# Low parts, conversion ends and splits go from GpSimd to VectorE in the network stage of an attention, expert and feed-forward kernel

## The chip, the cores and the metric

The kernel runs on 1 core of one Trainium2 chip. The metric is the device time of one execution in microseconds (us). Engines are named as in the profile: PE is TensorE's matmul, PEld its weight load, DVE is VectorE, ACT is ScalarE, POOL is GpSimd, SP is the engine that issues most DMAs (SPq is its queue of issues).

## What is computed

Three parts in a row, in float32, and the change touches the last one only:

```python
attn_out = _attn_ref(q, k, v, tau)                  # (4, 8, 576, 64), thresholded softmax
x = attn_out.transpose(0, 2, 1, 3).reshape(2304, 512)
x = _moe_ref(x, expert_emb, tau, w1, w2)            # one of 8 experts per token
def _moe2_ref(x, w_in, w_out, alpha):               # w_in 512 x 2048, w_out 2048 x 512
    h = x @ w_in
    g = np.maximum(h, 0.0) + alpha * np.minimum(h, 0.0)
    return (g @ w_out).astype(np.float32)
```

## The kernel before, in words

PE works here on float32 that is rounded to a shorter form (fp32r). To keep precision every operand is held as two such numbers: the **high part** is a cast (ACT), the **low part** is the operand less its high part, a subtraction. A product is then three matmuls: high by high, high by low, low by high.

The attention and the experts fill the first 608 us of the profiled execution and are not touched. The network stage, `near_network` (line 1804), is the rest. It makes six **visits** (`VISITS`, line 52), numbered 0 to 5: three blocks of 768 tokens, each with two halves of the 2048 hidden units, in an order that changes the block between visits 0 and 1, 1 and 2, 3 and 4, 4 and 5. A visit has four **passes** `i` (0 to 3). In a pass, seven products `p` in the order 1, 2, 6, 7, 5, 3, 4 (Strassen-like, `prod`, line 1877, six matmuls of 384 columns each) give four tiles of h. They go into two PSUM banks, `ha` and `hb`; between products ACT copies a partial sum out of `ha` (`held`, line 1890, tiles `v`, `w`, `d`), and the next product that accumulates into `ha` waits for that copy. `act` (line 1898) makes g from the sums with ACT and DVE, `halves` casts it (`gh`, line 1927), `low` subtracts on POOL (`gl`, line 1932), and `f2mm` (line 1979) multiplies by w_out.

Beside this three kinds of work prepare what comes later, each a **chain** of steps:

- `wout` and `win` (lines 2010 and 2037) convert float64 weights that are loaded as `cr`: `cvsteps` (line 1609) has ACT and DVE steps and, for w_out, two POOL steps at the end (lines 1627 and 1628); `win` ends with an addition on POOL (line 2053).
- `factors(i)` (line 2064), i from 4 to 7, makes the weight operands of visits 3 to 5 for one pass each: it loads `wa`, makes four sums on DVE (line 1698), and then for seven products a cast on ACT (line 2084), a low part on POOL (line 2088) and a store of the tile `wf` to `ws` in HBM (line 2090). `wf` has three buffers, so the fourth cast waits until the store of the first tile has landed, and so on.
- `fetch`, `diff` and `split` load the next block of tokens and make its seven operands x: `xsplit` (line 2101) casts on ACT and subtracts two halves on DVE or POOL.

The program's order is made while it is built. `tick(us)` (line 1846) is called after every product and every `f2mm`. It gives each engine `us` of room, up to a ceiling of 1.2, and lets chains take steps in the order of their rank (g first, then stores, fetch and x, then conversions, last the factors) as long as the step's engine has room left; a step takes its stated cost off the room. `finish(name)` (line 1836) puts all the steps that a chain still has into the program at once. `prod` calls it for factors when the next weight load, five products ahead, would need them:

```python
            if y2["wnext"][0] < len(y2["wseq"]):
                vv, ii, _ = y2["wseq"][y2["wnext"][0]]
                finish(("f", VISITS[vv][1] * NQH + ii))
            y2["weights"]()
```

Each engine executes its instructions in the order in which they were put, and SP issues DMAs in that order too: weight loads `wr<-ws`, the fetches `raw<-yt_d`, the loads `cr` and the stores `ws<-wf` share its queue.

Of the kernel before, what the change touches and what calls it, by code (L numbers as in the profile page):

```python
# [10 lines left out]
F32 = mybir.dt.float32  # L11
# [5 lines left out]
ALU = mybir.AluOpType  # L17
# [4 lines left out]
B, H, S, D = 4, 8, 576, 64  # L22
# [27 lines left out]
PROD = (1, 2, 6, 7, 5, 3, 4)  # L50
# [162 lines left out]
def attn_moe_ffn(ctx: ExitStack, tc, q, k, v, tau, emb, mtau, w1, w2, w_in, w_out, alpha, out):  # L213
    nc = tc.nc
# [134 lines left out]
    add = plan.add  # L349
# [1218 lines left out]
    def shared(st, general):  # L1568
# [37 lines left out]
            nc.sync.dma_start(raw.rearrange("p (k f) -> p k f", k=k) if k > 1 else raw, cvsource(which, c))  # L1606
            CV[which, c] = raw

        def cvsteps(raw, f, r, hl):

            raw = raw.rearrange("p (n w) -> p n w", w=2)
            lo, hi = raw[:, :, 0], raw[:, :, 1]
            ff, rf = f.bitcast(F32), r.bitcast(F32)
            A, V, G = nc.scalar, nc.vector, nc.gpsimd
            yield "A", 0.67, lambda: A.activation(ff, hi.bitcast(F32), AF.Abs)
            yield "V", 0.75, lambda: V.tensor_scalar(out=ff, in0=ff, scalar1=F64_TINY, scalar2=None, op0=ALU.max)
            yield "V", 0.75, lambda: V.tensor_scalar(out=f, in0=f, scalar1=3, scalar2=0x3FFFFFFF,
                                                     op0=ALU.logical_shift_left, op1=ALU.bitwise_and)
            yield "V", 1.2, lambda: V.scalar_tensor_tensor(out=f, in0=hi, scalar=0xC0000000, in1=f, op0=ALU.bitwise_and,
                                                           op1=ALU.bitwise_or)  # L1620
            if hl is not None:
                yield "A", 0.65, lambda: A.copy(hl[:, 0, :], ff)
            yield "V", 0.5, lambda: V.tensor_scalar(out=r, in0=f, scalar1=0xFF800000, scalar2=None, op0=ALU.bitwise_and)
            yield "V", 0.75, lambda: V.scalar_tensor_tensor(out=rf, in0=lo, scalar=2.0 ** -52, in1=rf, op0=ALU.mult,
                                                            op1=ALU.mult)
            if hl is not None:
                yield "P", 1.55, lambda: G.tensor_tensor(ff, ff, hl[:, 0, :].bitcast(F32), op=ALU.subtract)
                yield "P", 1.4, lambda: G.tensor_tensor(hl[:, 1, :], ff, rf, op=ALU.add)

        def conv():  # L1630

# [172 lines left out]
    def near_network(y2):  # L1804
# [41 lines left out]
        def tick(us):  # L1846

            now[0] += 1
            for e in room:
                room[e] = min(room[e] + us, 1.2)  # L1850
            for x in list(chains):
                last = None
                while x["steps"] and x["at"] < now[0]:
                    e, cost, fn = x["steps"][0]
                    if last not in (None, e) or room.get(e, 1) <= 0 or e == "W" and not fn():
                        break
                    x["steps"].pop(0)
                    if e == "W":
                        continue
                    fn()  # L1860
                    if e in room:
                        room[e] -= cost
                    last = e
                    if e == "N":
                        break
                if last is not None:
                    x["at"] = now[0]
                if not x["steps"] and x in chains:
                    chains.remove(x)
# [140 lines left out]
        def wout(c):  # L2010

            x = {}

            def load():
                open_.append(c)
                x["raw"] = raw = cw_p.tile([128, 1024], U32, tag="cr", name="cr", bufs=2)
                nc.sync.dma_start(raw, y2["cvsource"](2, c))

            def begin():
                f, r = (cw_p.tile([128, 512], U32, tag=nm, name=nm, bufs=2) for nm in ("f", "r"))  # L2020
                if c < NWO:
                    WO[c] = wo_p.tile([128, 2, DM], F32R, tag=f"wo{c}", name=f"wo{c}")
                else:
                    WO[c] = y2["cvp"].tile([128, 2, DM], F32R, tag=f"wo{c - NWO}", name=f"wo{c}", bufs=1)
                x["steps"] = [y[2] for y in y2["cvsteps"](x["raw"], f, r, WO[c])]
                x["steps"][0]()

            def nth(k):
                x["steps"][k]()
                if k == 8:  # L2030
                    open_.remove(c)

            kinds = [("V", 0.75), ("V", 0.75), ("V", 1.2), ("A", 0.65), ("V", 0.5), ("V", 0.75), ("P", 1.55), ("P", 1.4)]
            chain(3, [("W", 0, lambda: len(open_) < 2), ("S", 0, load)] + [("N", 0, nothing)] * 3 + [("A", 0.67, begin)]
                  + [(e, t, lambda k=k: nth(k + 1)) for k, (e, t) in enumerate(kinds)], ("wo", c))

        def win(c):

            x = {}

            def load():
                open_.append(("c", c))
                x["raw"] = raw = cw_p.tile([128, 1024], U32, tag="cr", name="cr", bufs=2)
                nc.sync.dma_start(raw.rearrange("p (k f) -> p k f", k=2), y2["cvsource"](1, c))

            def begin():
                f, r = x["fr"] = [cw_p.tile([128, 512], U32, tag=nm, name=nm, bufs=2) for nm in ("f", "r")]
                x["steps"] = [y[2] for y in y2["cvsteps"](x["raw"], f, r, None)]
                x["steps"][0]()

            def add():
                f, r = (t.bitcast(F32) for t in x["fr"])
                P.tensor_tensor(f, f, r, op=ALU.add)

            def store():
                i, half = divmod(c, 2)
                nc.sync.dma_start(wa_d[i - NQH][:, half * DM:(half + 1) * DM], x["fr"][0].bitcast(F32))
                open_.remove(("c", c))

            chain(3, [("W", 0, lambda: len(open_) < 2), ("S", 0, load)] + [("N", 0, nothing)] * 3 + [("A", 0.67, begin)]  # L2060
                  + [("V", t, lambda k=k: x["steps"][k + 1]()) for k, t in enumerate((0.75, 0.75, 1.2, 0.5, 0.75))]
                  + [("P", 1.4, add), ("N", 0, nothing), ("S", 0, store)], ("c", c))

        def factors(i):

            x = {}

            def load():
                made.append(i)
                for c in (2 * i, 2 * i + 1):  # L2070
                    finish(("c", c))
                x["wa"] = wa = y2["wa"].tile([128, 2, DM], F32, tag="wa", name="wa")
                nc.sync.dma_start(wa.rearrange("p x n -> p (x n)"), wa_d[i - NQH])

            def nth(k):
                if k == 0:
                    x["sums"] = y2["sums"](i, x["wa"])
                x["sums"][k](V)

            def next_(k):  # L2080

                if k < 7:
                    x[k] = t, _, _ = y2["wtile"](y2["wf"], "wf", i, PROD[k])
                    A.copy(t[:, 0].rearrange("p (k j) -> p k j", k=2), SUM[i][PROD[k]])
                    did("A", 0.42)
                if 1 <= k < 8:
                    h, l = (x[k - 1][0][:, y].rearrange("p (k j) -> p k j", k=2) for y in range(2))
                    P.tensor_tensor(l, SUM[i][PROD[k - 1]], h.bitcast(F32), op=ALU.subtract)
                if k >= 2:
                    nc.sync.dma_start(x[k - 2][2], x[k - 2][1])  # L2090
                if k == 8:
                    made.remove(i)

            steps = [("W", 0, lambda: not made and not any(x["name"] in (("c", 2 * i), ("c", 2 * i + 1)) for x in chains)),
                     ("S", 0, load)] + [("N", 0, nothing)] * 3
            steps += [("V", 0.8, lambda k=k: nth(k)) for k in range(4)] + [("N", 0, nothing)]
            for k in range(9):
                steps += [("P", 0.95, lambda k=k: next_(k))] + [("N", 0, nothing)] * (k % 2)
            chain(4, steps, ("f", i))

        def xsplit(p, e):
# [12 lines left out]
        def after(v, i, p):  # L2114

            if moving(v):
# [4 lines left out]
                if i == NQH - 1:  # L2121
                    finish("fetch")
                    if p in (1, 2, 6):
                        xsplit(p, {1: "V", 2: "P", 6: "V"}[p])
                    if p == 2:
                        chain(2, [("N", 0, nothing), ("P", 1.1, x4), ("P", 1.1, lambda: diff(4, P, 1))], ("d", 4))
                    if p == 7:
                        xsplit(7, "V")
                    if p == 5:
                        xsplit(5, "P")  # L2130
                    if p == 3:
                        xsplit(3, "V")
                    if p == 4:
# [2 lines left out]

        def x4():
            finish(("x", 1))
            diff(4, P, 0)

        work = {0: [("o", NV, 0), ("o", NV + 1, 0), ("o", NV + 2, 1), ("o", NV + 3, 2)],
                1: [("f", NQH, 0), ("c", 2 * NQH + 4, 0), ("f", NQH + 1, 1), ("c", 2 * NQH + 5, 1), ("o", 8, 2)],
# [1 line left out]
                    ("o", 11, 2), ("o", 12, 3)],  # L2144
                3: [("o", 13, 0), ("o", 14, 1), ("o", 15, 2)]}

        xsplit(3, "V")
        xsplit(4, "V")
        for v, (q, h) in enumerate(VISITS):
            for i in range(NQH):  # L2150
                pair = h * NQH + i
# [218 lines left out]
```

## Time and profile before

| | |
|---|---|
| time, median of 3 runs | 1007.3 us (1006.34 to 1008.09) |
| the profiled execution | 1008.7 us |
| its span, first to last instruction | 1006.9 us |
| PE busy over the span | 960.2 us (95%) |
| DVE busy | 811.4 us (81%) |
| ACT busy | 633.0 us (63%) |
| POOL busy | 673.3 us (67%) |

The busy share of PE says little about stalls of a microsecond: the ends of matmuls are modelled, and what counts is where PE waited, for what, and at which granted clock.

### The profile page before, as it was taken

What the parts mean: (1) busy time and instruction counts of PE and PEld (TensorE: products, weight loads), DVE (VectorE), ACT (ScalarE), POOL (GpSimd) and SP (SyncE); (2) the same over time, 40 slices, a digit from 0 to 9 for tenths busy, and PEclk for the clock granted to TensorE, in tenths of its full rate; (3) what the DMA queues carried; (4) which work ended last, traced back from release to release, by engine and by line L of the source; (5) the groups of instructions that cost most, each with busy time, mean ns of one, the idle gap of its engine ahead of it and who ended that gap; (6) DMA issues with size and microseconds to landing.
All of it is one profiled execution on the core that took longest, in us unless ns stands there. A gap on an engine that the chain in (4) does not pass through costs nothing. (4 is left out here: it accounts for less than half of the span.)

```text
span 1006.9 us, 18456 instructions
## 1 busy us (share of the span) xinstructions
PE 960.2 (95%) x6099; PEld 889.6 (88%) x6099; DVE 811.4 (81%) x1461; ACT 633.0 (63%) x1451; POOL 673.3 (67%) x663
## 2 busy tenths in 40 slices
PE   7999999899999599999998999999989999999996
PEld 6899999799999499999997997888878888898895
DVE  7999999999999767969889776886877879746543
ACT  6999989799998444646555565575665625526220
POOL 6989899899999601745778564574765857735523
PEclk9999999999999799999999899999999999999998
DMA  2333455535452286887878687558677676574551
GB/s 75 104 97 83 131 165 177 157 101 143 123 146 80 108 304 200 293 282 229 299 246 245 211 226 229 160 175 297 197 251 242 203 257 199 161 236 146 178 168 67
DMA packets 119451, 186.08 MB, mean 185 GB/s; under 512 B 24056, under 2 KB 50968, under 8 KB 119344
## 3 DMA queue, kind: packets, MB, share of 16 engines
q1 hardware_dynamic: 115472, 174.48, 55.8%
q0 software_dynamic: 3456, 9.59, 2.5%
q8 instruction: 51, 0.84, 0.4%
q10 hardware_dynamic: 416, 0.72, 0.2%
q14 instruction: 56, 0.46, 0.2%
HBM read 127.48 MB, written 48.41 MB: 175 GB/s over the span
## 5 line engine op out<-in xcount | busy, mean ns | idle before, releaser
L1932 POOL TENSOR_TENSOR gl<-c,gh 128x384 fp32r<-128x384 f32 x96 | 110.1, 1150 | 134.6 <-ACT gh L1927 100.1
L446 POOL TENSOR_TENSOR ptl<-x,pth 128x512 fp32r<-128x512 f32 x97 | 124.8, 1287 | 6.8
L650 DVE SCALAR_TENSOR_TENSOR p<-s,mx,e 128x576 f32<-128x576 f32 x144 | 116.6, 812 | 7.5 <-ACT mx L638 3.2
L1225 PE MATMUL l<-x,w 128*128 128x256 f32 (+6 forms) x744 | 120.0, 311 | 0.0
L1883 PE MATMUL ha<-x,wr 128*128 128x384 f32 x576 | 117.3, 338 | 2.8 <-ACT c L1910 2.2
L1999 PE MATMUL o<-wo,gh 128*128 128x512 f32 x288 | 113.3, 393 | 2.4 <-ACT gh L1927 2.4
L2001 PE MATMUL o<-wo,gl 128*128 128x512 f32 x288 | 114.3, 397 | 1.1 <-POOL gl L1932 1.1
L634 DVE TENSOR_REDUCE mx<-s 128x1 f32<-128x576 f32 x144 | 108.5, 754 | 8.1 <-PE s L627 4.9
L2000 PE MATMUL o<-wo,gh 128*128 128x512 f32 x288 | 114.0, 396 | 0.0
L663 PE MATMUL t<-ident,p 128*128 128x128 f32 (+1 forms) x720 | 111.9, 276 | 2.3 <-ACT x L689 1.0
L1883 PEld LDWEIGHTS ha<-x,wr 128*128 128x128 f32 x576 | 103.1, 188 | 12.1 <-ACT c L1910 2.7
L1225 PEld LDWEIGHTS l<-x,w 128*128 128x128 f32 x744 | 112.1, 190 | 0.6
L643 ACT ACTIVATE e<-s,mx 128x576 f32<-128x576 f32 x144 | 106.3, 739 | 7.2 <-DVE mx L634 6.0
L663 PEld LDWEIGHTS t<-ident,p 128*128 128x128 f32 (+1 forms) x720 | 80.8, 137 | 8.5 <-DVE p L650 2.3
L1883 PE MATMUL hb<-x,wr 128*128 128x384 f32 x432 | 87.8, 338 | 0.5 <-DVE c L1905 0.5
L1208 ACT ACTIVATE h<-l 128x256 fp32r<-128x256 f32 (+6 forms) x64 | 28.2, 441 | 95.2 <-PE l L1225 90.4
L1257 PE MATMUL y<-h,w 128*128 128x256 f32 (+6 forms) x256 | 80.7, 315 | 5.5 <-DVE h L1209 5.3
L627 PE MATMUL s<-ks,qs 128*128 128x288 f32 x256 | 82.7, 338 | 3.0 <-ACT qs L534 1.4
L1256 PE MATMUL y<-h,w 128*128 128x256 f32 (+6 forms) x256 | 82.7, 323 | 0.6 <-ACT h L1208 0.6
L1138 POOL TENSOR_TENSOR w<-stg,w 128x512 fp32r<-128x512 f32 x28 | 38.4, 1371 | 65.6 <-ACT w L1137 62.3
L1258 PE MATMUL y<-h,w 128*128 128x256 f32 (+6 forms) x256 | 79.8, 312 | 0.0
L1883 PEld LDWEIGHTS hb<-x,wr 128*128 128x128 f32 x432 | 76.9, 190 | 1.5 <-DVE c L1905 1.5
(277 smaller groups left out, 2689.3 us busy)
## 6 DMA issues: line engine op xcount, KB each, us to landing
wr<-ws SPq DMA_DIRECT2D x168, 256.0 KB
stg<-in_moe_w_dram SPq DMA_DIRECT2D x34, 512.0 KB
stg<-in_moe_w_dram SPq DMA_DIRECT2D x15, 1024.0 KB
kx<-ks SPq DMA_DIRECT2D x60, 144.0 KB
xd<-zt SPq DMA_DIRECT2D x33, 256.0 KB
raw<-yt_d SPq DMA_DIRECT2D x10, 768.0 KB
ws<-wr SPq DMA_DIRECT2D x28, 256.0 KB
ws<-wf SPq DMA_DIRECT2D x28, 256.0 KB
```

The lines of the kernel that those rows point to most:

```text
L446: lambda: nc.gpsimd.tensor_tensor(lo, raw, hi.bitcast(F32), op=ALU.subtract))
L627: nc.tensor.matmul(s[:, hf, 0:288], lt, st[nm, a][:, hf * 288:(hf + 1) * 288], start=(j == 0 and x == 0), stop=(j == n - 1 and x == 1))
L634: nc.vector.tensor_reduce(out=mx[:, 0:1], in_=st["s", t][:, :, 0:288], op=ALU.min, axis=AX.XY)
L643: nc.scalar.activation(e, st["s", t][:, :, 0:288], AF.Exp, bias=st["mx", t][:, 0:1], scale=-1.0)
L650: nc.vector.scalar_tensor_tensor(out=p.rearrange("q (a b) -> q a b", a=2), in0=st["s", t][:, :, 0:288], scalar=st["mx", t][:, 2:3], in1=st ...
L663: nc.tensor.transpose(m[0:w, j * n + i * 128:j * n + (i + 1) * 128], st["p", t][:, c * 128:c * 128 + w], ident)
L1225: nc.tensor.matmul(m[:, 0:n], w[:, a, c], st["x"][:, b, c, 0:n], start=(i == 0), stop=(i + 1 == len(terms)))
L1883: nc.tensor.matmul(m, w[:, a, k], x[:, b, k], start=start and n == 0, stop=n + 1 == len(terms), skip_group_check=not start)
L1932: P.tensor_tensor(gl, c, gh.bitcast(F32), op=ALU.subtract)
L1999: nc.tensor.matmul(m, gh[:, ts], WO[f][:, 0, :], start=first and x == 0, stop=False)
L2000: nc.tensor.matmul(m, gh[:, ts], WO[f][:, 1, :], start=False, stop=False)
L2001: nc.tensor.matmul(m, gl[:, ts], WO[f][:, 0, :], start=False, stop=n[0] == full and x + 1 == len(gs))
```

## The change

Every subtraction or addition that POOL did for conversions, for factors and for the splits and differences of x in the network stage is put on DVE; the stated costs of these steps go down. POOL keeps `low` (gl) and the stores of the result by index. The ceiling of the room goes from 1.2 to 2.1. The splits of x 3 and 4 ahead of the first visit are finished before the first product is put.

```diff
-        def cvsteps(raw, f, r, hl):
+        def cvsteps(raw, f, r, hl, end="P"):
...
-            A, V, G = nc.scalar, nc.vector, nc.gpsimd
+            A, V = nc.scalar, nc.vector
+            G = V if end == "V" else nc.gpsimd
...
-                yield "P", 1.55, lambda: G.tensor_tensor(ff, ff, hl[:, 0, :].bitcast(F32), op=ALU.subtract)
-                yield "P", 1.4, lambda: G.tensor_tensor(hl[:, 1, :], ff, rf, op=ALU.add)
+                yield end, 1.55, lambda: G.tensor_tensor(ff, ff, hl[:, 0, :].bitcast(F32), op=ALU.subtract)
+                yield end, 1.4, lambda: G.tensor_tensor(hl[:, 1, :], ff, rf, op=ALU.add)
...
-                room[e] = min(room[e] + us, 1.2)
+                room[e] = min(room[e] + us, 2.1)
...
-                x["steps"] = [y[2] for y in y2["cvsteps"](x["raw"], f, r, WO[c])]
+                x["steps"] = [y[2] for y in y2["cvsteps"](x["raw"], f, r, WO[c], "V")]
...
-            kinds = [("V", 0.75), ("V", 0.75), ("V", 1.2), ("A", 0.65), ("V", 0.5), ("V", 0.75), ("P", 1.55), ("P", 1.4)]
+            kinds = [("V", 0.75), ("V", 0.75), ("V", 1.2), ("A", 0.65), ("V", 0.5), ("V", 0.75), ("V", 0.65), ("V", 0.65)]
...
-                P.tensor_tensor(f, f, r, op=ALU.add)
+                V.tensor_tensor(f, f, r, op=ALU.add)
...
-                  + [("P", 1.4, add), ("N", 0, nothing), ("S", 0, store)], ("c", c))
+                  + [("V", 0.65, add), ("N", 0, nothing), ("S", 0, store)], ("c", c))
...
-                    P.tensor_tensor(l, SUM[i][PROD[k - 1]], h.bitcast(F32), op=ALU.subtract)
+                    V.tensor_tensor(l, SUM[i][PROD[k - 1]], h.bitcast(F32), op=ALU.subtract)
...
-                steps += [("P", 0.95, lambda k=k: next_(k))] + [("N", 0, nothing)] * (k % 2)
+                steps += [("V", 0.45, lambda k=k: next_(k))] + [("N", 0, nothing)] * (k % 2)
...
-                        xsplit(p, {1: "V", 2: "P", 6: "V"}[p])
+                        xsplit(p, "V")
                     if p == 2:
-                        chain(2, [("N", 0, nothing), ("P", 1.1, x4), ("P", 1.1, lambda: diff(4, P, 1))], ("d", 4))
+                        chain(2, [("N", 0, nothing), ("V", 0.5, x4), ("V", 0.5, lambda: diff(4, V, 1))], ("d", 4))
...
-                        xsplit(5, "P")
+                        xsplit(5, "V")
...
-            diff(4, P, 0)
+            diff(4, V, 0)
...
-        xsplit(3, "V")
-        xsplit(4, "V")
+        for p in (3, 4):
+            xsplit(p, "V")
+            finish(("x", p))
```

The order of PE's instructions does not change. What the table of steps makes of the others is seen at three places. A line of the changed kernel is one higher than the same line before.

**ACT in visit 1, pass 1**, from the copy of w to the copy of d. Before:

```order
L1892 COPY w<-ha 128x384
L2084 CAST wf<-wa 128x256
L1615 ACTIVATE f<-cr 128x512
L2084 CAST wf<-wa 128x256
L1927 CAST gh<-c 128x384
L1892 COPY d<-ha 128x384
```

and now:

```order
L1893 COPY w<-ha 128x384
L1616 ACTIVATE f<-cr 128x512
L2085 CAST wf<-sum 128x256 x2
L1928 CAST gh<-c 128x384
L1893 COPY d<-ha 128x384
```

The casts of the third and the fourth factor tile stand ahead of the copy of d; before, the first and the second stood there.

**ACT and SP in visit 3, pass 1**, where factor 6 ends (before, it had ended in pass 0, and the casts below were those of factor 7). ACT before, from the copy of v:

```order
L1892 COPY v<-ha 128x384
L1927 CAST gh<-c 128x384
L1892 COPY w<-ha 128x384
L1927 CAST gh<-c 128x384
L1615 ACTIVATE f<-cr 128x512
L1892 COPY d<-ha 128x384
L2084 CAST wf<-wa 128x256 x2
L2084 CAST wf<-sum 128x256 x2
```

and now:

```order
L1893 COPY v<-ha 128x384
L2085 CAST wf<-sum 128x256
L1928 CAST gh<-c 128x384
L2085 CAST wf<-sum 128x256 x3
L2085 CAST wf<-wa 128x256
L1893 COPY w<-ha 128x384
L1928 CAST gh<-c 128x384
```

SP in the same place before, from the fetch of the next block:

```order
L1731 DMA raw<-yt_d 128x2x768 x2
L2017 DMA cr<-in_moe_w_out_dram 128x1024
L1726 DMA wr<-ws 128x512 x5
L2090 DMA ws<-wf 128x512 x2
L1726 DMA wr<-ws 128x512
```

and now:

```order
L1732 DMA raw<-yt_d 128x2x768 x2
L2018 DMA cr<-in_moe_w_out_dram 128x1024
L2091 DMA ws<-wf 128x512
L1727 DMA wr<-ws 128x512
L2091 DMA ws<-wf 128x512 x6
```

The last five casts of factor 6 (the third to the seventh) stand between the copies of v and w, and all its seven stores behind the fetch.

**ACT in visit 3, pass 2**, where factor 7 ends. Before, between the copies of v and w:

```order
L1892 COPY v<-ha 128x384
L1927 CAST gh<-c 128x384
L1622 CAST wo_11448<-f 128x512
L2084 CAST wf<-sum 128x256
L1909 ACTIVATE u<-c 128x384
L1910 ACTIVATE c<-c 128x384
L2084 CAST wf<-wa 128x256
L1892 COPY w<-ha 128x384
```

and now:

```order
L1893 COPY v<-ha 128x384
L1928 CAST gh<-c 128x384
L1910 ACTIVATE u<-c 128x384
L1911 ACTIVATE c<-c 128x384
L2085 CAST wf<-wa 128x256 x2
L2085 CAST wf<-sum 128x256 x4
L2085 CAST wf<-wa 128x256
L1893 COPY w<-ha 128x384
```

All seven casts of factor 7 stand there in one row, where two stood.

## Rows read from the trace of the kernel before

**Rows 1.** Busy time of each engine by stretch: start:end us, length, then busy (instructions), clock, DMA.

```profile
608.00:865.00 257.00, 250.20 (x1228) 221.28 (x1227) 207.74 (x269) 150.06 (x309) 160.03 (x136) 0.99 0.68 220
849.00:990.00 141.00, 141.00 (x702) 126.58 (x702) 82.68 (x123) 55.95 (x108) 70.38 (x64) 1.00 0.54 164
...
753.00:759.00 6.00, 5.75 (x21) 4.83 (x22) 4.29 (x7) 5.07 (x12) 3.66 (x5) 0.72 0.87 305
...
553.00:562.00 9.00, 8.50 (x39) 8.50 (x40) 7.47 (x12) 4.28 (x10) 5.25 (x5) 0.63 0.57 214
```

**Rows 2.** Who waited for whom in the network stage: us in total, times, longest.

```profile
ACT wf L2084 <- DMA ws<-wf: 10.9, 6, 3.6
...
PE o L1999 <- ACT gh L1927: 2.4, 3, 1.3
PE ha L1883 <- ACT c L1910: 2.2, 1, 2.2
...
PE o L2001 <- POOL gl L1932: 1.1, 3, 0.4
PE hb L1883 <- DVE c L1905: 0.5, 1, 0.5
```

**Rows 3.** Timeline where PE stood: start us, us, what, [idle before, and its end].

```profile
553.50 0.63 PE L1257 MATMUL y<-h,w 128*128 128x320 f32 x1 [3.04 <-DVE h L1209]
...
704.06 0.50 PE L1999 MATMUL o<-wo,gh 128*128 128x512 f32 x1 [1.26 <-ACT gh L1927]
...
752.02 0.40 ACT L2084 CAST wf<-sum 128x256 fp32r<-128x256 f32 x1 [3.61 <-DMA ws<-wf]
...
753.25 1.52 PE L1883 MATMUL ha<-x,wr 128*128 128x384 f32 x6 [2.22 <-ACT c L1910]
```

**Rows 4.** Groups of instructions in the network stage: count, busy us, mean ns, idle before.

```profile
L1756 DVE TENSOR_TENSOR x<-raw,x 128x384 fp32r<-128x384 f32 x36 | 29.7, 858 | 0.0
...
L1627 POOL TENSOR_TENSOR f<-f,wo 128x512 f32<-128x512 f32 x12 | 19.4, 1618 | 7.4 <-DVE r L1623 3.5 <-ACT f L1615 2.6 <-PE o L2001 0.9
...
L2088 POOL TENSOR_TENSOR wf<-sum,wf 128x256 fp32r<-128x256 f32 x16 | 14.7, 919 | 5.9 <-ACT wf L2084 5.9
```

**Rows 5.** Timeline of DVE: two subtractions with no POOL instruction beside them.

```profile
740.13 0.54 DVE L1756 TENSOR_TENSOR x<-raw,x 128x384 fp32r<-128x384 f32 x1
...
824.05 0.42 DVE L1698 TENSOR_TENSOR sum<-wa 128x256 f32<-128x256 f32 x1
```

**Rows 6.** Timeline of visit 3, pass 1: SP's issues, ACT, PE's product 5.

```profile
816.29 1.21 SPq L1731 DMA_DIRECT2D raw<-yt_d  x2
817.60 0.54 SPq L2017 DMA_DIRECT2D cr<-in_moe_w_out_dram  x1
...
823.31 0.48 ACT L1892 COPY w<-ha 128x384 f32<-128x384 f32 x1 [3.29 <-PE ha L1883]
...
826.18 1.23 PE L1883 MATMUL ha<-x,wr 128*128 128x384 f32 x6
...
826.48 0.67 ACT L1615 ACTIVATE f<-cr 128x512 f32<-128x512 f32 x1 [2.08 <-DMA cr<-in_moe_w_out_dram]
...
829.13 1.33 SPq L2090 DMA_DIRECT2D ws<-wf  x2
...
831.23 0.41 ACT L2084 CAST wf<-sum 128x256 fp32r<-128x256 f32 x1 [2.34 <-DMA ws<-wf]
```

**Rows 7.** Timeline of visit 1, pass 1: a store, PE's product 3, the fourth cast.

```profile
691.95 6.38 SPq L2090 DMA_DIRECT2D ws<-wf  x2
...
696.28 1.29 PE L1883 MATMUL ha<-x,wr 128*128 128x384 f32 x6
...
698.39 0.41 ACT L2084 CAST wf<-sum 128x256 fp32r<-128x256 f32 x1 [0.35 <-DMA ws<-wf]
```

**Rows 8.** Timeline of the stage's start: the casts of x 3 and 4, product 6.

```profile
610.64 1.69 ACT L1752 CAST x<-raw 128x768 fp32r<-128x768 f32 x2
...
610.80 1.31 PE L1883 MATMUL ha<-x,wr 128*128 128x384 f32 x6
```

## The prediction

> **What bounds the kernel now.** I read the windows first. In the part of the network stage that the change touches, 608 to 865 us, PE is busy 250.2 of 257.0 us and DVE 207.7 [rows 1]. In the quiet part behind it, 849 to 990 us, PE is busy for the whole stretch at full clock: 702 matmuls, 78 to a pass, so a pass without a stall takes 141 / 9 = 15.67 us. PE sets the pace, then, and can't go faster; only its stalls can come or go. Against 15.67 us a pass the stage loses about 12 us by my count. The chain of waits says for whom [rows 2]: ACT's cast of a factor tile `wf` stands 10.9 us in six waits for stores to land, and PE waits for ACT, for POOL and for DVE in smaller pieces. The timeline shows how the first becomes the second [rows 3]: at 752.02 a cast has waited 3.61 us for a store, the copy that PE needs sits behind it on ACT, and PE starts at 753.25 after 2.22 us of nothing. At 704.06 PE has lost 1.26 us to a late `gh`.
>
> A stall has a second price. In the window 753 to 759, behind the idle 2.22 us, the mean granted clock is 0.72 where 1.00 is 2.4 GHz; in 553 to 562, behind an idle 3.04 us, it is 0.63 [rows 1, 3]. The lower of the two levels is 1.2 GHz. The work lost is 6 x 0.28 = **1.7 us** and 9 x 0.37 = **3.3 us**. I charge 1.7 for a stall between 2 and 3 us and 3.3 for a longer one.
>
> **Part one: 80 instructions come to DVE.** By the diff these are 24 ends of w_out (512 columns), 4 additions of w_in (512), 28 low parts of factors (256), 16 halves of x splits and 8 differences (384). Alone on the chip a DVE subtraction takes 0.54 us for 384 columns and 0.42 for 256 [rows 5]; for 512 I scale 0.54 x 512/384 = 0.72, an estimate. Sum: 28 x 0.72 + 28 x 0.42 + 24 x 0.54 = 45 us of DVE work. POOL loses about 100 us (at 1.62 us for 512 columns, 0.92 for 256, some 1.2 for 384 between them). While POOL works, DVE's own subtractions take 858 ns on average against 540 alone [rows 4, 5], so 37% of such time is waiting for POOL; of 100 us that is 37 us that DVE gets back. DVE ends 8 us up, near 216 of 257. Beside PE, that is covered: **0**. If the cover is gone (DVE pays the price with POOL for everything), this is rival D.
>
> **Part two: what goes.** With POOL nearly free and DVE's steps shorter, the waits `PE ha <- ACT c` (2.2), the longest `PE o <- ACT gh` (1.3), the longest `<- POOL gl` (0.4) and `PE hb <- DVE c` (0.5) of [rows 2] go; with the first goes its clock loss, 1.7, and about 0.4 of slow restarts: **-6.5**. What is late next at 704 and 753 is PE itself. Bounds: -3 (only the 753 stall without its clock loss, and some of the rest) to -8.
>
> **Part three: the start.** The splits of x 3 and 4 are now forced ahead of product 1, so ACT makes both casts, 1.69 us [rows 8], before the first copy `v`; before, the copy came first. Product 6, at 610.80, needs the copy: +1.5. Two later waits of PE for `gh` there soak up about 1.0. **+0.5**, bounds 0 and 1.5.
>
> **Part four: the factors come too late.** This is the main term, and it rests on the order. Factors have the lowest rank; their low parts now want DVE's room, where all chains compete, and no longer POOL's, which was idle. So `finish` finds them with many steps left: factor 6 in visit 3, pass 1 and factor 7, whole, in pass 2. Forced steps are put in one row on ACT ahead of the copy that the next product needs. With three buffers, each fourth cast waits for a store to land, and behind it on ACT stand `gh`, the activations of g and the copy; PE waits for the copy.
>
> *Factor 6 (visit 3, pass 1).* All seven stores are now behind the fetch of the next block and the load `cr` in SP's queue. The trace shows such a place: the fetch is issued at 816.29, `cr` at 817.60, and `cr` is used only at 826.48 [rows 6]. A store issued behind them lands then, I take it, and cast 4 runs at 826.5. From there one turn of the ring: cast 0.41, low part 0.42, about 0.4 until SP issues it (a choice, somewhat more than half of an issue, 1.33 for two), landing 2.1 (829.13 to 831.23). So cast 7 can start at 829.8 and ends at 830.2, the copy of w, 0.48, at 830.7. PE needs it at 826.18: **+4.5, and 3.3 by the clock**. Bounds: 0 if stores don't queue behind the fetch; 6.4 if each store takes 6.38 - 2.1 more, less what overlaps.
>
> Here a rule speaks against me. The trace shows a store landing 6.4 us after its issue where loads stood ahead of it, 691.95 to 698.39 [rows 7], and 2.1 us where nothing did [rows 6]. The Trainium skill, "DMA: Bandwidth & Descriptors", section "Anatomy of one DMA — SWDGE (gpsimd) path", has a DMA take about 2.0 us plus its bytes at 436 GB/s, which for 256 KB is 2.6 us by estimate, with no term for what was issued before; by it factor 6 would cost nothing and the sum would be 7.8 lower. The first row goes against that rule and the second with it, so it stands as rival B.
>
> *Factor 7 (visit 3, pass 2).* Seven casts in a row: two turns of the ring, 2 x 3.3, and the last cast, 0.4: 7.0 us. ACT can begin early: ahead of the copy of w in pass 1 it idles 3.29 us [rows 6], of which a cast and two activations, now ahead of the row, take three times some 0.55, leaving 1.6. The copy has 2.4 of slack (823.31 + 0.48 against 826.18). 7.0 - 1.6 - 2.4 = **+3.0, and 3.3 by the clock**. Bounds: 2.3 (a faster turn) to 4.5 (no early start).
>
> *Factor 4 (visit 1, pass 1).* Casts 3 and 4 stand ahead of the copy of d. Cast 4 needs store 1, which before landed at 698.39 [rows 7]; now one load fewer is ahead of it, and I take 697.7. Then cast 0.41, `gh` 0.5, copy 0.48: 699.1 against product 3 at 696.28: **+2.8, and 1.7 by the clock**. Bounds: 0 (landing 2.1 us after 691.95) and 3.5 (landing at 698.39).
>
> **The sum:** 0.5 + 4.5 + 3.3 + 3.0 + 3.3 + 2.8 + 1.7 - 6.5 = +12.6 us. The profiled execution took 1008.7, so a like one would take 1021.3; it lies 1.4 above the median of the runs, and against the median of 1007.3 the forecast is **1019.9 us**. Low and high ends of the terms, clock losses included where a stall is left: about +3 and +19, so case A's own range is 1010 to 1026.
>
> **Rivals.**
>
> *B, stores land quickly (same).* If a store doesn't wait for the fetch issued ahead of it, factors 4 and 6 cost nothing and only factor 7 stalls: 0.5 + 6.3 - 6.5 = +0.3, 1007.6 us. For it: 2.1 us at 829.13 [rows 6]. Against it: 6.4 us at 691.95 [rows 7], and ACT's 3.61 us at 752 [rows 3].
>
> *C, no forced wait reaches PE (faster).* The stalls of part four would all have to fit into the slack of the copies, as four of the six waits for `ws` seem to today [rows 2]; then only the gains are left: 1007.3 - 6.5 = 1000.8 us. It decides where the row of casts takes less than 4.0 us (1.6 early, 2.4 slack) instead of 7.0. For it: DVE and POOL work one after the other today, 858 against 540 ns [rows 4, 5], and a free DVE makes the steps ahead come sooner. Of this lock the Trainium skill tells under "SBUF — State Buffer", section "Who interferes with whom": DVE and GpSimd share one pair of ports, held exclusively; the trace agrees, with those two durations. Against it: two landings of 2.1 us each stand in the row whatever DVE does.
>
> *D, DVE becomes the bound (much slower).* If the moved work is paid at the price with POOL, 45 x 858/540 = 71 us on 207.7 make 279 in 257 us [rows 1]: +22, 1029 us. It decides where DVE's busy time passes PE's. For it: DVE is at 81% there already. The Trainium skill, "Perfetto Trace Analysis", section "Optimizing Scalar/DVE Operations", would rather offload from a saturated DVE, even to GpSimd, though it doubts the gain for the shared port; by it this change goes the wrong way; no run yet shows which. Against it: POOL is left with `gl` alone, so little is contended.
>
> That the change doesn't do what it says is excluded by the order: the casts stand where I say. What isn't in it is when they wait.
>
> **How the numbers follow.** Case A 0.69, B 0.11, C 0.13, D 0.07. A change of 0.2%, 2 us, is about what a measurement of this kernel can tell from none. Faster: C and a little of B, 0.15. Same: most of B, 0.07. Slower: A, D and the rest of B, 0.78. The range runs from 1006.0, which takes in B, to 1026.0, the upper end of A; left out are C and D, 0.20.
>
> **What would show it.** In the profile of the changed kernel: the waits of ACT's `wf` casts for `ws` go up from 10.9 to about 20 us with a longest over 5; PE waits for a late copy `w` (`PE ha <- ACT w`) 3 to 5 us in each of visit 3's passes 1 and 2, each with a stretch at half clock behind it, and for `d` in visit 1's pass 1; the stalls at 704 and 753 are gone; POOL's busy time falls by about 100 us to some 570, and DVE's stays near 815. Wrong would be the forecast if PE does not stand in visit 3 (B or C), if the store behind the fetch lands well ahead of 826, or if PE waits for DVE at the splits of x instead (D). If the stalls stand where I say and the time is off, the landing times are the mis-sized term.

## The result and the profile after

The changed kernel takes 1021.64 us (median of 4 runs, 1018.23 to 1023.8) against 1007.18 us of the kernel before: a ratio of 1.0139 (95% interval 1.0119 to 1.0158), so slower by more than the interval. The profiled execution took 1023.8 us, 2.2 above the median; its span is 1022.0 us.

The profile of the changed kernel shows busy times by engine (us, share of the span, instructions):

```profile
PE 967.1 (95%) x6099; PEld 897.0 (88%) x6099; DVE 801.9 (78%) x1541; ACT 635.0 (62%) x1451; POOL 580.1 (57%) x583
```

DVE has taken over the work of 80 instructions and is busy 9.5 us *less* than before; POOL is busy 93 us less. The groups of DVE instructions in the network stage (count, busy us, mean ns) show where that comes from:

```profile
L1912 DVE SCALAR_TENSOR_TENSOR c<-u,na,c 128x384 f32<-128x384 f32 x64 | 44.1, 690 | 9.0 <-ACT c L1911 8.7
L1757 DVE TENSOR_TENSOR x<-raw,x 128x384 fp32r<-128x384 f32 x44 | 29.0, 712 | 2.1 <-ACT x L1753 2.1
...
L2089 DVE TENSOR_TENSOR wf<-sum,wf 128x256 fp32r<-128x256 f32 x16 | 8.9, 560 | 14.7 <-ACT wf L2085 14.6
```

The split of x, 858 ns before [rows 4], is 712 ns now (44 instructions instead of 36, eight of the moved ones among them), and the step of g, the first line, that took 967 ns on average in the kernel before takes 690. The Trainium skill, "SBUF — State Buffer", section "Who interferes with whom", has DVE and GpSimd share one pair of ports that one of them holds at a time. These durations agree: instructions of the same shape got 17 and 29% shorter when POOL had less to do.

So it is not DVE's or POOL's work that costs. The list of waits (us in total, times, longest) tells what does:

```profile
ACT wf L2085 <- DMA ws<-wf: 21.5, 10, 7.3
...
PE ha L1884 <- ACT w L1893: 8.5, 2, 5.1
...
PE ha L1884 <- ACT d L1893: 5.6, 3, 2.9
...
PE ha L1884 <- ACT v L1893: 1.6, 1, 1.6
...
PE o L2002 <- POOL gl L1933: 0.7, 2, 0.3
...
PE o L2000 <- ACT gh L1928: 0.3, 1, 0.3
```

Against [rows 2], the casts wait twice as long for stores, PE now waits for the copies w, d and v, and the waits for `gh`, `c` and `hb` are almost gone. In the windows (columns as in [rows 1]; the last is GB/s moved by DMA) the stalls can be placed; the stretch behind them is as quiet as before:

```profile
612.80:618.60 5.80, 5.21 (x18) 4.58 (x18) 1.91 (x4) 1.93 (x5) 0.00 (x0) 0.71 0.67 194
...
766.00:772.00 6.00, 3.86 (x20) 3.21 (x19) 2.88 (x6) 3.67 (x9) 1.02 (x1) 1.00 0.56 200
834.00:839.50 5.50, 5.46 (x14) 4.74 (x15) 4.28 (x9) 2.59 (x5) 1.27 (x2) 0.50 0.94 310
855.00:860.00 5.00, 4.11 (x13) 3.52 (x14) 3.20 (x7) 3.40 (x7) 1.01 (x1) 0.67 0.76 274
702.00:706.00 4.00, 3.71 (x13) 3.71 (x14) 3.34 (x7) 2.31 (x6) 1.00 (x1) 0.63 0.27 64
```

```profile
865.00:1005.00 140.00, 140.00 (x699) 125.75 (x698) 80.76 (x137) 55.22 (x106) 52.54 (x49) 1.00 0.54 165
```

The first row is the start, the others factors 5, 6, 7 and 4. And the longest stall, in visit 3, pass 1, on the timeline (start us, us, what, idle before and its end):

```profile
818.90 1.21 SPq L1732 DMA_DIRECT2D raw<-yt_d  x2
820.22 0.53 SPq L2018 DMA_DIRECT2D cr<-in_moe_w_out_dram  x1
820.85 0.56 SPq L2091 DMA_DIRECT2D ws<-wf  x1
...
830.28 0.40 ACT L2085 CAST wf<-sum 128x256 fp32r<-128x256 f32 x1 [7.34 <-DMA ws<-wf]
831.54 0.40 ACT L2085 CAST wf<-sum 128x256 fp32r<-128x256 f32 x1 [0.86 <-DMA ws<-wf]
832.13 0.41 ACT L2085 CAST wf<-sum 128x256 fp32r<-128x256 f32 x1 [0.19 <-DMA ws<-wf]
833.21 0.40 ACT L2085 CAST wf<-wa 128x256 fp32r<-128x256 f32 x1 [0.67 <-DMA ws<-wf]
833.52 0.47 ACT L1893 COPY w<-ha 128x384 f32<-128x384 f32 x1
...
834.04 2.29 PE L1884 MATMUL ha<-x,wr 128*128 128x384 f32 x6 [5.08 <-ACT w L1893]
```

A store issued 0.63 us behind `cr` and 1.9 us behind the fetch lands after 9.4 us (a landing is counted from the issue to the start of the cast that waited for it). The cast waits for it, the copy of w stands behind four casts, and PE behind the copy.

Where the 15.1 us between the two spans (1022.0 - 1006.9) arise is read from the starts of the same product in both traces, since PE's order is the same. The difference of the starts grows or shrinks like this (0.3 us are there when the stage begins, and the end gives 0.3 back). Both traces are of one execution each.

| stretch | difference before and behind it | worth |
|---|---|---|
| start, visit 0, passes 0 and 1 | 0.27 to 2.94 | +2.7 |
| factor 4 (visit 1, pass 1) | 2.94 to 7.59 | +4.65 |
| the old stall at 704 | 7.59 to 5.44 | -2.15 |
| the old stalls from 735 to 757 | 5.45 to 0.18 | -5.3 |
| factor 5 (visit 2, pass 1) | 0.18 to 2.61 | +2.4 |
| factor 6 (visit 3, pass 1) | 2.61 to 10.46 | +7.85 |
| factor 7 (visit 3, pass 2) | 10.46 to 15.37 | +4.9 |

### The profile page after: what moved, and what is told of

Its sections match the earlier page's. It is cut to its first block, busy times and chain, and to the rows that moved or that the text cites. A ratio compares the mean times of both kernels' runs of the same rounds, so it can differ in the third digit from the quotient of the medians.

```text
span 1022.0 us, 18439 instructions
## 1 busy us (share of the span) xinstructions
PE 967.1 (95%) x6099; PEld 897.0 (88%) x6099; DVE 801.9 (78%) x1541; ACT 635.0 (62%) x1451; POOL 580.1 (57%) x583
## 5 line engine op out<-in xcount | busy, mean ns | idle before, releaser
L1884 PE MATMUL ha<-x,wr 128*128 128x384 f32 x576 | 119.8, 344 | 15.7 <-ACT w L1893 8.5
L707 PE MATMUL v<-pth,hlv 128*128 128x288 f32 (+2 forms) x256 | 75.9, 318 | 2.2 <-DVE run L953 1.0
```

The costliest lines, as they stand in the source:

```text
L1884: nc.tensor.matmul(m, w[:, a, k], x[:, b, k], start=start and n == 0, stop=n + 1 == len(terms), skip_group_check=not start)
```

## The experiments

The change has two sides: the *order* (the table of steps, with its costs and its room) and the *engine* (who executes the 80 instructions). The theory is that the order costs all of it, through factors that come too late for a ring of three `wf` buffers, and that the engine gives a little. Rival D is that the engine costs. The order has three edits in it, the costs and rooms of the steps, the ceiling and the `finish` at the start; the ceiling was not tried alone. Ratios are against the kernel before, run beside each group on the same chip.

### Order and engine apart

`e1`: the kernel before, its table as it was, and only the instructions on DVE:

```diff
-        ENG = {"V": V, "P": P}
+        ENG = {"V": V, "P": V}
-                    P.tensor_tensor(l, SUM[i][PROD[k - 1]], h.bitcast(F32), op=ALU.subtract)
+                    V.tensor_tensor(l, SUM[i][PROD[k - 1]], h.bitcast(F32), op=ALU.subtract)
...
```

> The order of the kernel before, with the 80 instructions on VectorE: the placement alone. Theory (the loss is the late factors, the move itself relieves DVE of POOL): no forced row longer than the four steps of before, DVE's subtractions faster; part of the gains (the waits for ACT c, gh, gl, hb) comes, the wait of a cast for its store near 750 may stay: 1003 us, between 999 and 1006. Rival D (45 us more on DVE make it the bound): PE waits for DVE at the splits of x, 1010 us or more.

Measured: 0.9985 (0.9969 to 1.0001), 1003.6 us, inside the theory's range. `e2`: the changed kernel's table, and the instructions back on POOL (the reverse edit).

> The order of the changed kernel, with the 80 instructions on POOL as before: the order alone. Theory: all four stalls at factors 4 to 7 stay and are no shorter, since a low part takes 0.9 us instead of 0.45 in every turn of the ring: 1021.6 plus 2 to 6, so 1024 to 1028 us, with waits of the wf casts for ws over 20 us. Rival D (the placement is what costs): back to 1007 to 1011 us.

Measured: 1.0205 (1.0178 to 1.0232), 1024.56 us, as the theory had it. Together with the kernels before and after this makes a square:

| | instructions on POOL | on DVE |
|---|---|---|
| order of before | 1 | 0.9985 |
| order of the change | 1.0205 | 1.0139 |

The order costs 16 us with DVE and 21 with POOL; the engine gives 1.5 us in the old order, where the interval just reaches 1, and some 7 in the new one. (The lower right cell comes from a group of runs of its own; the intervals are 0.002 to 0.003 either way, so the 7 can be anything from 3 to 10.) Rival D falls: e1 is not slower, and its instructions on DVE are as short as after the change, while those of e2 are long. The groups of DVE in the network stage, e1 and then e2:

```profile
L1912 DVE SCALAR_TENSOR_TENSOR c<-u,na,c 128x384 f32<-128x384 f32 x64 | 44.3, 693 | 10.7 <-ACT c L1911 10.4
```

```profile
L1912 DVE SCALAR_TENSOR_TENSOR c<-u,na,c 128x384 f32<-128x384 f32 x64 | 56.3, 881 | 16.5 <-ACT c L1911 15.9
```

In e2 the waits of the casts are as long as after the change, so the stalls don't depend on where the low part is taken:

```profile
ACT wf L2085 <- DMA ws<-wf: 21.3, 10, 6.9
```

What e2 has on top are two waits of PE for a low part of g from POOL, 4.1 us, that the changed kernel has not:

```profile
657.88 0.50 PE L2002 MATMUL o<-wo,gl 128*128 128x512 f32 x1 [2.35 <-POOL gl L1933]
...
867.70 0.50 PE L2002 MATMUL o<-wo,gl 128*128 128x512 f32 x1 [1.73 <-POOL gl L1933]
```

### Why the factors are late

`e4`: the factors draw on POOL's room again, executed on DVE as in the change:

```diff
-                steps += [("V", 0.45, lambda k=k: next_(k))] + [("N", 0, nothing)] * (k % 2)
+                steps += [("P", 0.95, lambda k=k: next_(k))] + [("N", 0, nothing)] * (k % 2)
```

> The changed kernel, but the factors' steps draw on POOL's room at 0.95 as before, while the instruction stays on VectorE. Theory: no factor is finished by force, the stalls of factors 4 to 7 (19.8 us with their clock, by the products' starts) go, the start's 2.7 stays: 1002 us, between 1000 and 1006; waits of the wf casts for ws under 12 us. Rival (with DVE loaded, the stall goes elsewhere: PE waits for low parts of x or for gh): 1010 us or more.

Measured: 1.0004 (0.9979 to 1.0029), 1004.26 us: 13.5 us of the loss are gone with one line of the table. The theory gave 19.8; as a ratio its range was 0.993 to 0.999, and the measured one lies above it. What is missing is factor 4, whose stall is still there (the one at the start was meant to stay):

```profile
ACT wf L2085 <- DMA ws<-wf: 8.6, 7, 2.5
...
PE ha L1884 <- ACT d L1893: 2.9, 3, 2.1
```

In e4 the casts of the third and fourth tile stand ahead of the copy of d in visit 1, pass 1, as in the changed kernel; in the kernel before ACT had come only to the first and second there. So factor 4 is not late in the changed kernel but further on, and DVE's room is not what moved it. Nor is it forced: in the changed kernel `finish` finds 7 steps of factor 6 left, 16 of factor 7, with all its casts, and none of factors 4 and 5; in e4 and e9 it finds none of any factor. Which entry of the table moved factor 4 stays open; the higher ceiling is a candidate. By the products' starts factor 4 costs 3.9 us in e4's trace and 1.9 in that of e6 below. The first is of an execution of 1007.72 us, 3.5 above e4's median, the second of one 3.4 below e6's, so what it costs in a run between is known only roughly.

`e9`: the factors stay in DVE's room, but in the rank of the conversions, and the start is as before:

```diff
-            chain(4, steps, ("f", i))
+            chain(3, steps, ("f", i))
...
-            finish(("x", p))
```

> The changed kernel without the forced splits at the start, and with the factors in the rank of the conversions instead of below it, their steps drawing on VectorE's room as in the changed kernel. Theory (it is the low rank in a room that all chains use that makes the factors late): no factor is finished by force, the stalls in visit 3 go, ratio 0.996 to 1.000; conversions of w_out come later instead, which should cost nothing. Rival (VectorE's room is too small for all of it, whoever comes first): PE waits for wo or for factors, ratio over 1.003.

Measured: 1.0003 (0.9992 to 1.0014), just above the theory's range and under the rival's. The stalls of visit 3 are gone, but another has come near 693, at factor 4, though nothing is forced there: a cast meets a store that is still behind the fetch of visit 1, again with a copy behind it on ACT:

```profile
ACT wf L2085 <- DMA ws<-wf: 12.5, 7, 7.9
...
PE ha L1884 <- ACT w L1893: 4.8, 1, 4.8
```

So the force is not what costs by itself. What costs is a cast that waits for a store and stands ahead of a copy.

### The ring

`e3`: the changed kernel with four buffers of `wf`; a buffer of `u` is given up for the room.

```diff
-        y2["wf"] = npool("wf", bufs=3)
+        y2["wf"] = npool("wf", bufs=4)
-            u = c_p.tile([128, HB], F32, tag="u", name="u", bufs=3)
+            u = c_p.tile([128, HB], F32, tag="u", name="u", bufs=2)
```

> The changed kernel, with four buffers of wf instead of three (and two of the tile u instead of three, which pays for the room). Theory (the ring of three sets the stalls): casts 3 and 4 of factors 4 and 5 wait for no store, so those two stalls go (4.6 and 2.4 us with their clock); factor 7 has one turn instead of two (3 to 5 us); factor 6 still waits for its first store, but has two casts fewer behind it (1 to 2 us). Sum 11 to 14 us: ratio 1.000 to 1.005 against the kernel before. Rival (what stops the casts is not the ring but ACT or VectorE behind the forced steps): ratio 1.011 to 1.016.

Measured: 1.0031 (1.0019 to 1.0043), inside the theory's range. Some 11 us go with one buffer, in an order that is otherwise the same; the stalls left are those of factors 6 and 7, smaller:

```profile
ACT wf L2085 <- DMA ws<-wf: 9.9, 5, 6.1
...
PE ha L1884 <- ACT w L1893: 4.9, 2, 3.2
```

### What a store waits for

`e8`: POOL issues the factors' stores, so they stand behind nothing in SP's queue.

```diff
-                    nc.sync.dma_start(x[k - 2][2], x[k - 2][1])
+                    P.dma_start(x[k - 2][2], x[k - 2][1])
```

> The changed kernel, with the stores ws<-wf of the factors issued by POOL instead of SP; all else as it was. Theory A (a store lands behind the fetch because it stands behind it in SP's queue of issues): the first store of factor 6 lands 2 to 4 us after its issue instead of 9.4, PE's stall of 5.1 us in visit 3, pass 1 falls under 1.5, and the time by 5 to 9 us, to a ratio of 1.004 to 1.010 against the kernel before. Rival (the transfers themselves share the 16 engines, whichever queue issues them): the casts still wait over 5 us, ratio 1.012 to 1.016.

Measured: 1.0121 (1.01 to 1.0142): theory A fails for factor 6, and the time is in the rival's range. The timeline of this kernel, with the fetch at 809.25:

```profile
809.25 1.21 SPq L1732 DMA_DIRECT2D raw<-yt_d  x2
810.57 0.53 SPq L2018 DMA_DIRECT2D cr<-in_moe_w_out_dram  x1
...
810.88 0.56 POOL L2091 DMA_DIRECT2D ws<-wf  x1
...
818.52 0.41 ACT L2085 CAST wf<-sum 128x256 fp32r<-128x256 f32 x1 [5.23 <-DMA ws<-wf]
```

The store still takes 7.6 us from its issue, and the ring turns more slowly: from cast 4 to cast 7 it is 5.0 us (818.52 to 823.52) where the changed kernel takes 2.9. So PE's stall at factor 6 is what it was, 5.05 us. Moving the stores does help factors 4 and 5: by the products' starts their stalls shrink to 0.5 us and to nothing. In the changed kernel SP was held there by weight loads that waited for PE to be done with a buffer, at factor 4 3.15 us for two of them ahead of the stores:

```profile
690.31 3.15 SPq L1727 DMA_DIRECT2D wr<-ws  x2
693.55 1.95 SPq L2091 DMA_DIRECT2D ws<-wf  x2
```

What is gained there is lost at factor 7, where PE stands 5.9 us instead of 3.4 with POOL as issuer:

```profile
PE ha L1884 <- ACT w L1893: 11.0, 2, 5.9
```

`e10`: the two fetches of visit 3 are left out.

```diff
-                    chain(2, [("S", 0, lambda: fetch(VISITS[v + 1][0], 0)), ("S", 0, lambda: fetch(VISITS[v + 1][0], 1))]
+                    chain(2, ([("S", 0, lambda: fetch(VISITS[v + 1][0], 0)), ("S", 0, lambda: fetch(VISITS[v + 1][0], 1))] if v != 3 else [("S", 0, nothing)] * 2)
```

> The changed kernel without the two fetches of 768 KB in visit 3 (the last two visits then multiply stale tokens); SP's other issues stand as they did. Theory (in e8 the first store of factor 6, issued by POOL behind the fetch, still took 7.6 us: the store shares the DMA engines with the fetch's bytes): store 1 lands 2 to 4 us after its issue instead of 9.4, PE's stall at product 5 of visit 3, pass 1 falls from 5.1 to under 2 us with little half clock behind it, factor 7's stall stays: 5 to 8 us less, ratio 1.006 to 1.009 against the kernel before. Rival (the weight loads and cr ahead of it are what delays the store): stall over 3.5 us, ratio 1.011 or more.

Measured: 1.0047 (1.0031 to 1.0062), 9 us less than with the fetch: a little more than the theory said, since the stall of factor 6 is gone altogether. Its timeline:

```profile
813.09 0.37 SPq L2018 DMA_DIRECT2D cr<-in_moe_w_out_dram  x1
813.52 0.42 SPq L2091 DMA_DIRECT2D ws<-wf  x1
...
818.70 0.41 ACT L2085 CAST wf<-sum 128x256 fp32r<-128x256 f32 x1 [1.62 <-DMA ws<-wf]
```

5.2 us from the issue, with `cr` still ahead, not the 2 to 4 expected. So of the 9.4 us that store 1 took, the fetch makes some 4, and the place in SP's queue about 2 (9.4 against 7.6). Why a store without the fetch takes 5.2 us and not the 2.1 of [rows 6] was not taken apart. The Trainium skill, "DMA: Bandwidth & Descriptors", section "Anatomy of one DMA — SWDGE (gpsimd) path", would have 2.6 us for such a store by estimate, and its heading says that it is about DMAs that GpSimd issues. In e8, where POOL issues the store, it took 7.6; only the 2.1 us of [rows 6] come near the estimate, and the measurement decides.

### The start

`e5`: the changed kernel without `finish(("x", p))` ahead of the first product.

> The changed kernel without the forced splits of x 3 and 4 at the start. Theory: the first copy comes ahead of the two casts again, and the 2.7 us that the start has lost come back, the stalls of the factors stay: 1019 us, between 1018 and 1020.5. Rival (the start's delay is hidden by later waits): 1021 to 1022 us.

Measured: 1.011 (1.0076 to 1.0143), 0.0029 or 2.9 us less than the change as a whole, against 2.7 read from the products' starts. The two intervals overlap, so the times alone don't show it. By the products' starts in e5's trace the start is worth -0.9 us against the kernel before, where the changed kernel has +2.7. `e6` joins this with e4's line:

> The changed kernel with both repairs: the factors' steps draw on POOL's room, and no forced splits at the start. Theory (the effects add): the run with the first repair alone had a ratio of 1.0004, the second was worth 0.003: ratio 0.997, between 0.995 and 0.999. Rival (they overlap: the start's delay is taken up by later waits once the stalls are gone): 1.000.

Measured: 0.9986 (0.9975 to 0.9997), inside the theory's range; the rival's 1.000 lies just outside the interval. Against e4 it is 1.8 us less, but e4's interval is 2.5 us either way, so that the two effects add is likely and not shown.

### Versions that beat both

The ring of four, alone on the kernel before, then with each of the better versions:

> The kernel before, order and engines as they were, with four buffers of wf and two of the tile u. Theory (the ring is what costs the kernel before its stall near 750, 2.2 us and 1.7 by the clock): the waits of the wf casts for ws fall from 10.9 to under 6 us, the stall goes: ratio 0.996 to 0.998. Rival (late DVE and POOL steps hold the casts just as long): 0.999 to 1.001.

> The order of the kernel before with the 80 instructions on VectorE (as in the first run, ratio 0.9985) and the ring of four. Theory (the two effects add): its stalls of 1.5 and 1.2 us near 747 and 700 go or shrink: ratio 0.994 to 0.997. Rival (both remove the same wait): 0.997 to 0.999, as with one of them alone.

> The changed kernel with the factors on POOL's room, without the forced splits at the start, and with the ring of four. Theory: its one stall left at a factor, 1.8 us near 693 for a store, goes: 2 us less than the ratio 0.9986 of the run without the ring, so 0.996 to 0.998. Rival (with two u buffers DVE and ACT wait for each other instead): 0.998 to 1.001.

Measured: `e11` 0.9955 (0.9939 to 0.9971), `e12` 0.9945 (0.9929 to 0.9961), `e13` 0.994 (0.992 to 0.996), 1000.21 us in the middle of its runs. In e11 nothing but two buffer counts differs from the kernel before; the casts' waits for stores fall from 10.9 us to

```profile
ACT wf L2084 <- DMA ws<-wf: 0.7, 1, 0.7
```

and 4.5 us go, at the upper edge of what was expected or a little beyond. On e6 the ring is worth as much, 4.6 us in e13, more than the theory gave. What DVE adds on top of the ring (e12 against e11) is 1 us, inside the intervals, so that it adds at all is not shown, though e12 lies in its theory's range; and the difference of e13 to both is inside them too.

## Why the prediction was right

The forecast was 1019.9 us, slower, with a range of 1006 to 1026; measured are 1021.64. Its two largest costs, factors 6 and 7, were right for the reason it gave: casts in a row that wait for stores, with a copy behind them. That the sum came so close is luck in part: it lacked 4.6 us at the start and at factor 5, and had 2.3 too much at factor 7 and in what goes. The measured terms are of one execution, 2.2 us above the median.

| step | forecast, clock included | measured |
|---|---|---|
| start | +0.5 | +2.7 |
| factor 4 | +4.5 | +4.65 |
| factor 5 | 0 | +2.4 |
| factor 6 | +7.8 | +7.85 |
| factor 7 | +6.3 | +4.9 |
| what goes | -6.5 | -7.4 |

- **DVE's 45 us at nothing:** right, by e1 and by the square. "DVE ends 8 us up" had the wrong sign: DVE's busy time fell by 9.5 us, so the instructions that were there already gave back more than the 37 us worked out. The 858 ns are the mean of all 36 splits, not of those beside POOL, so "while POOL works" misread the row.
- **Factor 6, "a store issued behind them lands then, I take it":** the time was nearly right, 11.4 us from the fetch to cast 4 instead of 10.2; e10 shows that the fetch is the largest part of the cause, and e8 that it is its bytes more than the place in the queue. The turn from cast 4 to cast 7 took 2.93 us (830.28 to 833.21) where 3.3 was worked out. PE stood 5.08 us instead of 4.5, and the clock took 2.75 instead of 3.3, so that the term as a whole agrees within 0.1 is luck.
- **Factor 4:** the size was right (PE stood 2.9 us where 2.8 was worked out, and 702 to 706 at 0.63 is 1.5 by the clock), and so was the wait of cast 4 for a store. "Too late" was not: by e4 this factor runs further on than before, whatever room it draws on.
- **Factor 7:** the row of seven casts took 7.4 us (848.02 to 855.46) where 7.0 was worked out, and PE stood 3.4 us where 3.0 was. The clock was charged with 3.3; 855 to 860 at 0.67 is 1.65. That is where the term was too large. First and last of the row:

```profile
848.02 0.70 ACT L2085 CAST wf<-wa 128x256 fp32r<-128x256 f32 x2
...
855.06 0.40 ACT L2085 CAST wf<-wa 128x256 fp32r<-128x256 f32 x1 [1.24 <-DMA ws<-wf]
```

- **The start was mis-sized.** PE stood 1.65 us, about as worked out (1.5), but "two later waits soak up about 1.0" failed, and a loss by the clock was not charged: 612.8 to 618.6 at 0.71 is 1.7 us.
- **Factor 5 was missed.** Its stores stand behind three weight loads that occupy SP for 4.5 us from 756.46; store 1, issued at 762.56 behind them and a load `cr`, lets cast 4 go at 767.79, ahead of the copy of d. The prediction had no term for it. So the old stall near 750 did not go: it came back as this one, 2.1 us of idle PE.

```profile
756.46 4.50 SPq L1727 DMA_DIRECT2D wr<-ws  x3
...
762.56 0.93 SPq L2091 DMA_DIRECT2D ws<-wf  x2
...
767.79 0.40 ACT L2085 CAST wf<-sum 128x256 fp32r<-128x256 f32 x1 [5.60 <-DMA ws<-wf]
```

- **What goes:** the size was right, the reason was not. I put it down to POOL and DVE being freed. In e1, where they are freed in the old order, the waits for `gh` and `c` stay:

```profile
PE o L2000 <- ACT gh L1928: 2.9, 4, 1.0
...
PE ha L1884 <- ACT c L1911: 1.3, 1, 1.3
```

In e2, where they are not freed but the order is new, the first is down to 0.3 us and the second is gone. So the new order took these stalls away. What made them in the old one was the ring: e11 takes 4.5 us from them with more buffers and no move at all. At 752 the cast waited 3.61 us for a store, and behind it stood the activation `c`, not a copy, that PE waited for [rows 3]; the late `gh` at 704 stood behind such a cast too, in the kernel before:

```profile
703.19 0.40 ACT L2084 CAST wf<-sum 128x256 fp32r<-128x256 f32 x1 [2.72 <-DMA ws<-wf]
703.50 0.51 ACT L1927 CAST gh<-c 128x384 fp32r<-128x384 f32 x1
```

- **The range:** the terms' own ends, added up with their clock losses, give about -4 and +23 us, not the "+3 and +19" from which 1010 to 1026 was taken.
- **Rivals:** B lacks the stall of factor 6, C all of them, and D expected waits for DVE; `PE hb <- DVE c` is not among PE's waits any more.

Not wholly settled is why the old order gains only 1.5 us from DVE and the new one 7: the two waits for `gl` that e2 has and the changed kernel has not make 4.1 of it, and the rest lies within the intervals.

## What to carry to other kernels

A change of engine in a program that a planner orders (here `tick` with its table of costs) is two changes; build the old order with the new engine, and the new order with the old one, before saying which of them moved the time. Where an engine executes in order, look for an instruction that waits for a buffer ahead of one that PE waits for: its cost is not its duration but the landing of the slowest DMA that frees the buffer, and one buffer more can be worth more than the whole change of engines. And a store's landing time is that of its place: here 2.1 us where only one weight load was issued shortly ahead of it [rows 6], 9.4 behind a fetch of 1.5 MB and a load of 0.5 MB.

## What the runs showed of the hardware

TensorE's granted clock did not follow the length of the stall. After an idle 1.65 us at 611 the granted clock was 0.71 over the next 5.8 us; after an idle 2.14 us at 767, the mean of 766 to 772 was 1.00; after 5.08 us it was 0.50 over 5.5 us (1.2 GHz throughout, 2.75 us lost), and after the 3.4 us at 852 it was 0.67 over 5 us. The prediction's two prices, 1.7 and 3.3 us by the length of the stall, were thus right on average at best.
